# Clustered attention and two MLPs on one core: another order of the work of the first heads

## The chip, the core and the metric

The kernel runs on one core of one Trainium2 chip. The metric is the device time of one execution in microseconds (us). The engines are named as in the profile: PE is TensorE's matmul, PEld its load of weights, DVE is VectorE, ACT ScalarE, POOL GpSimd, SP SyncE, whose queue issues most DMAs. Each engine takes its instructions strictly in the order in which the program emits them.

## The reference, cut to what matters

```
q_assign = argmax(q_n . c_n); k_assign = argmax(k_n . c_n)      # 16 clusters per head, unit vectors
mask   = q_assign[:, :, :, None] == k_assign[:, :, None, :]
scores = where(mask, scale * (q @ k.T), -1e9)                   # 2 batches x 8 heads, seq 768, head_dim 64
attn   = exp(scores - max(scores)); attn /= sum(attn) + 1e-9
x      = (attn @ v) as [1536, 512]
x      = (g where h = x @ w_in, g = h * sigmoid(1.702 h)) @ w_out            # d_ff 2048
out    = (silu(x @ w_gate) * (x @ w_val)) @ w_out                            # d_ff 1536
```

## The kernel before

Sixteen (batch, head) pairs, here simply heads 0 to 15 as in the code, go through attention one after the other; then come the MLPs, which are dense matmuls. The change touches only heads 0 to 4, that is the first 60 us of 864.

What one head needs, with the names of the code:

- `load_qk(h)` (L309, SP queue) brings q and k, transposed, into one of four staging tiles. `hi_q`, `hi_k` (L321, L325, L326, on ACT) write their fp32r-rounded part into the operand tiles `q2(h)`, `k2(h)`, and `lo_q`, `lo_k` (L330, L336, on DVE, or on POOL where the call says so) write the remainder beside it. `extra_rows(i)` (L369, L370) is three POOL memsets that prepare the rows of an operand tile which hold the clusters and the maxima.
- `similar` (L431) is eight matmuls for one head, q and k against the centroids, into one tile of `ps_x`, which has a single buffer. `largest` (L451 to L460) and `assign` (L469 to L480) turn that, on DVE, into one-hot rows; the last step transposes half of the sequence at a time (L477) and two copies per half (L480, on the engines that the call names) put the rows into `q2(h)` and `k2(h)`.
- `smax(h, c, n, pool, tag)` is one matmul on those rows (L503) and one DVE maximum over its PSUM tile (L508), twelve times per head. They give an upper bound of the scores of a row; `mneg` (L519, DVE) and `mrow` (matmul L535, ACT copy L537, a small DMA L538) put its negative into `q2(h)`. For head 0 `mrow_at_once` does that in two halves without the DMA (L526, L530).
- `scores(h, c, n)` is two matmuls (L550) and one ACT exponential (L557); `pv(h, c)` (L566) is the product with the values, twelve matmuls. `ps_m` has two PSUM buffers, `ps_s` three, `ps_o` two. `keep_warm` (L353) issues matmuls on zeros.

The schedule is written out by hand: the order of emission is the order on each engine. In the loop over heads (L654 on), head h's twelve scores are mixed with the twelve `smax` of head h + 1, and then six `pv(h, c)` follow, with other work hung on their c. Head 0 is special: its scores come ahead of the loop, together with the first six `smax` of head 1. Then, in the loop at h = 0, ACT gets `hi_q(4)` and `hi_k(4)`, DVE gets `lo_q(4)` and `lo_k(4)` at c = 0, and then come the last six `smax` of head 1, two behind each of `pv(0, 0)` to `pv(0, 2)`. At c = 3 come `mneg(1)`, `similar([2])`, `mrow(1)`, `largest([2])` and `assign([2])`. The loop at h = 1 opens with the first `scores(1, ...)` and `smax(2, ...)`.

Of the kernel before, what the change touches and what calls it, by code (L numbers as in the profile page):

```python
# [25 lines left out]
def tile_cluster_attention_two_mlps(ctx: ExitStack, tc: tile.TileContext, qk, v, cen, w1, w2, wg, wv, w3, out):  # L26
    nc = tc.nc
    B, H, D, _, S = qk.shape
# [243 lines left out]
    with ExitStack() as att:  # L272
# [34 lines left out]
        def load_qk(h):  # L307
            b, hh = divmod(h, H)
            nc.sync.dma_start(out=stage[h % NST], in_=qk[b, hh])  # L309
# [9 lines left out]
        def hi_q(h):  # L319
            src = stage[h % NST][:, 0:1, :]  # L320
            nc.scalar.copy(q2(h)[0:D], src.to_broadcast([D, 2, S]))  # L321

        def hi_k(h):
            src = stage[h % NST][:, 1, :]
            nc.scalar.copy(k2(h)[0:D, 1, :], src)  # L325
            nc.scalar.copy(k2(h)[D:2 * D, 0, :], src)  # L326

        def lo_q(h, eng=nc.vector):
            t = q2(h)
            eng.tensor_tensor(  # L330
                out=t[D:2 * D, 0, :], in0=stage[h % NST][:, 0, :], in1=t[0:D, 0, :].bitcast(F32), op=ALU.subtract
            )

        def lo_k(h, eng=nc.vector):
            t = k2(h)
            eng.tensor_tensor(  # L336
                out=t[0:D, 0, :], in0=stage[h % NST][:, 1, :], in1=t[0:D, 1, :].bitcast(F32), op=ALU.subtract
            )
# [28 lines left out]
        def extra_rows(i):  # L367
            for t in (q2_t[i], k2_t[i]):
                nc.gpsimd.memset(t[D:MROW, 1, :].bitcast(F32), 0.0)  # L369
            nc.gpsimd.memset(k2_t[i][MROW:MROW + 1, 1, :].bitcast(F32), 1.0)  # L370
# [8 lines left out]
        for i in range(NC):  # L379
            nc.vector.memset(wd[:, :, i:i + 1], float(NC - i))  # L380
        nc.gpsimd.memset(v_t[0][:, :, D:D + 1], 1.0)
        for i in range(1, 4):
            extra_rows(i)


# [38 lines left out]
        def similar(hs):  # L424


            ps = ps_x.tile([128, HALF], F32, tag="x", name="sims")
            todo = [(i, a, j, h, n) for n in range(2) for j, h in enumerate(hs) for i in (1, 0) for a in (0, 1)]
            for at, (i, a, j, h, n) in enumerate(todo):
                o = LEAD + 128 * (h % H) - (64 * n + 32 * i + NC * j)  # L430
                nc.tensor.matmul(  # L431
                    out=ps,
                    lhsT=cs[:, (1 + i) * a, o:o + 128],
                    rhs=(q2, k2)[i](h)[:, 0, n * HALF:(n + 1) * HALF],
                    start=(at == 0),
                    stop=(at == len(todo) - 1),
                )
            return ps
# [53 lines left out]
        def do(steps):  # L492
            for _ in steps:
                pass
# [15 lines left out]
        def next_smax(h, todo):  # L510
            c, n = todo.pop(0)
            smax(h, c, n, *((ps_m, "m"), (ps_m, "m"), (ps_x, "x"))[(len(todo) + 1) % 3])
# [8 lines left out]
        def mrow_at_once(h, n, pl, tag):  # L521

            ps = pl.tile([128, 512], F32, tag=tag, name="mrow1")[MROW:MROW + 1, 0:HALF]
            for c in range(SC // 2):
                at = n * (SC // 2) + c
                nc.tensor.matmul(  # L526
                    out=ps[:, c * 128:(c + 1) * 128], lhsT=nr_t[h][:, at:at + 1].bitcast(F32), rhs=ident,
                    start=(c == 0), stop=(c == SC // 2 - 1), skip_group_check=True,
                )
            nc.scalar.copy(q2(h)[MROW:MROW + 1, 1, n * HALF:(n + 1) * HALF], ps)  # L530

        def mrow(h, pl=ps_x, tag="x"):

            ps = pl.tile([SC, 128], F32, tag=tag, name="mrow")
            nc.tensor.matmul(out=ps, lhsT=nr_t.pop(h), rhs=ident_r)  # L535
            row = sm_p.tile([SC, 128], F32R, tag="row", name="row")
            nc.scalar.copy(row, ps)  # L537
            nc.sync.dma_start(  # L538
                out=q2(h)[MROW:MROW + 1, 1, :].rearrange("p (c s) -> p c s", s=128).bitcast(F32), in_=row.bitcast(F32)
            )  # L540
# [3 lines left out]
        def scores(h, c, n):  # L544
            if n == 0:
                p_t[h, c] = p_p.tile([128, S], F32, tag="p", name="p")
            at = slice(n * HALF, (n + 1) * HALF)
            ps = ps_s.tile([128, 512], F32, tag="s", name="st")[:, 0:HALF]
            for a, rows in ((0, 2 * D), (1, MROW + 1)):
                nc.tensor.matmul(  # L550
                    out=ps,
                    lhsT=k2(h)[0:rows, a, c * 128:(c + 1) * 128],
                    rhs=q2(h)[0:rows, a, at],
                    start=(a == 0),
                    stop=(a == 1),
                )
            nc.scalar.activation(p_t[h, c][:, at], ps, ACTF.Exp, scale=scale)  # L557
# [66 lines left out]
        hi_k(2)  # L624
        hi_q(2)
        lo_k(2, nc.gpsimd)
        load_qk(4)
        for i, (c, n) in enumerate((c, n) for m in range(2) for n in range(2) for c in range(3 * m, 3 * m + 3)):
            smax(0, c, n, *((ps_m, "m"), (ps_m, "m"), (ps_s, "s"), (ps_s, "s"), (ps_s, "s"))[i % 5])
            keep_warm(1)  # L630
            if i == 5:
                mneg(0, slice(0, SC // 2))
        mrow_at_once(0, 0, ps_o, "o")
        mneg(0, slice(SC // 2, SC))
        sims = similar([1])
        for c in range(SC):
# [2 lines left out]
        do(assign([1], (nc.vector.tensor_copy, nc.gpsimd.tensor_copy)))  # L639
        lo_q(2, nc.gpsimd)  # L640
        mrow_at_once(0, 1, ps_o, "o")
        maxima = [(c, n) for c in range(SC) for n in range(2)]
        for c in range(SC):
            scores(0, c, 1)
            next_smax(1, maxima)
        hi_k(3)
        hi_q(3)
        lo_k(3, nc.gpsimd)
# [7 lines left out]
        for h in range(NH):  # L656
            more, ahead = h + 1 < NH, h + 4 < NH
            if h > 0:
                maxima = list(steps) if more else []
            for step in steps if h else ():  # L660
                scores(h, *step)
                if maxima:
                    next_smax(h + 1, maxima)
            if h == 0:
                load_qk(5)
            if ahead:
                hi_q(h + 4)
                if h == 0:
                    hi_k(h + 4)
            if 0 < h < NH - 1:  # L670
                mneg(h + 1)
            if h % 2 == 0 and 0 < h < NH - 3:
                do(assign([h + 2, h + 3]))
            if h == NH - 1:
                qk_stack.close()
                sp_p = pool(ctx, "sp", 5, side="right")
                g_p = pool(ctx, "gp", 3, side="right")
                w_pools.append(pool(ctx, "wd1", LATE, side="right"))
            for c in range(SC):
                pv(h, c)  # L680
                if more and c == 0:
                    if h > 0:
                        mrow(h + 1)
                    load_v(h + 1)
                    if ahead:
                        if h > 0:
                            hi_k(h + 4)
                        lo_q(h + 4)
                        lo_k(h + 4)
                        if h + 6 < NH:  # L690
                            load_qk(h + 6)
                        if h + 5 == NH:
                            qk1_stack.close()
                            stage_stack.close()
                            for to, t in zip((xh, xl), new_x(pool(ctx, "x1", 1, side="right"), 1)):
                                to.append(t)
                            w_pools.append(pool(ctx, "wd0", MID, side="right"))
                if h == 0:
                    for _ in range(min(2, len(maxima))):
                        next_smax(1, maxima)  # L700
                    if c == 3:
                        mneg(1)
                        sims = similar([2])
                        mrow(1, ps_o, "o")
                        do(largest([2], sims))
                        do(assign([2], (nc.scalar.copy, nc.vector.tensor_copy)))
                if h == 1 and c == 1:
                    do(largest([3], similar([3])))
                    do(assign([3]))
                if h > 0 and c == 0:  # L710
                    norm(h - 1)
                if h == NH - 1 and c > 0:
                    run([], [[("1", 0)], [("1", 1), ("2", 0)], [("1", 2)], [("2", 1)], []][c - 1], 0)
                take(takes.get((h, c), 0))
                if h == 1 and c == 4:
                    fetch_to(2)
                if h % 2:
                    if c == 2 and ahead:
                        do(largest([h + 3, h + 4], similar([h + 3, h + 4])))
                    if c in (3, 4) and h > 2:  # L720
                        to_x((h - 3) // 2, c - 3)
            if h == NH - 1:
                norm(h)
# [72 lines left out]
```

## Time and profile before

| | us |
|---|---|
| median of 3 runs | 865.94 (865.82 to 865.94) |
| the profiled execution, its own time | 865.92 |
| its span in the trace | 864.0 |
| PE busy in the span | 850.7 |
| DVE / ACT / POOL busy | 586.7 / 432.5 / 28.9 |

The profiled execution lies at the median, and its span is 1.9 us shorter than its time. Times in the rows are microseconds from the start of the span. Busy shares are means over stages with different limits; what the first heads are worth is read from their own stretch.

### The profile page before, as it was taken

What the parts mean: (1) busy time and instruction counts of PE and PEld (TensorE: products, weight loads), DVE (VectorE), ACT (ScalarE), POOL (GpSimd) and SP (SyncE); (2) the same over time, 40 slices, a digit from 0 to 9 for tenths busy, and PEclk for the clock granted to TensorE, in tenths of its full rate; (3) what the DMA queues carried; (4) which work ended last, traced back from release to release, by engine and by line L of the source; (5) the groups of instructions that cost most, each with busy time, mean ns of one, the idle gap of its engine ahead of it and who ended that gap; (6) DMA issues with size and microseconds to landing.
All of it is one profiled execution on the core that took longest, in us unless ns stands there. A gap on an engine that the chain in (4) does not pass through costs nothing.

```text
span 864.0 us, 12943 instructions
## 1 busy us (share of the span) xinstructions
PE 850.7 (98%) x5096; PEld 765.9 (89%) x5096; DVE 586.7 (68%) x1125; ACT 432.5 (50%) x819; POOL 28.9 (3%) x43
## 2 busy tenths in 40 slices
PE   8799999999999999999999999999999999999998
PEld 6699999999999988888888888888888888888886
DVE  7677878888896468888887767687774344333433
ACT  6546776676665445565664545564433233222322
POOL 9400000000000000000000000000000000000000
PEclk9889999999999999999999999999999999999999
DMA  5112222221122023333222222222200010000001
GB/s 114 34 27 71 90 54 56 60 51 50 35 81 76 1 84 112 109 111 119 101 74 82 67 97 74 74 74 75 96 1 1 1 49 25 1 1 1 0 1 74
DMA packets 26192, 49.73 MB, mean 58 GB/s; under 512 B 14522, under 2 KB 14612, under 8 KB 26132
## 3 DMA queue, kind: packets, MB, share of 16 engines
q1 hardware_dynamic: 25188, 47.14, 18.1%
q10 hardware_dynamic: 944, 1.77, 0.6%
q8 instruction: 40, 0.66, 0.3%
q14 instruction: 20, 0.16, 0.1%
HBM read 45.12 MB, written 3.15 MB: 56 GB/s over the span
## 4 chain that ended last, share of the span: by engine, by line
PE 94%; DVE 3%; POOL 2%; ACT 1%; issue 0%; DMA 0%; DVEq 0%; POOLq 0%; SPq 0%
PE h L156 39%; PE a L156 27%; PE pv L566 13%; PE st L550 7%; PE smax L503 4%; PE sims L431 3%; DVE nm L508 1%; PE xt L595 1%; POOL k L369 0%; POOL q L369 0%; POOL cs L365 0%; ACT q L321 0%; PE warm L353 0%; POOL k L370 0%; DVE oT L477 0%
## 5 line engine op out<-in xcount | busy, mean ns | idle before, releaser
L156 PE MATMUL h<-xh,sp 128*128 128x512 f32 (+1 forms) x1280 | 327.1, 337 | 0.1
L156 PEld LDWEIGHTS h<-xh,sp 128*128 128x128 f32 x1280 | 223.2, 189 | 28.4 <-issue 0.3
L156 PE MATMUL h<-xl,sp 128*128 128x256 f32 (+1 forms) x640 | 215.9, 337 | 0.0
L188 DVE SCALAR_TENSOR_TENSOR t<-t,h 128x512 f32<-128x512 f32 x112 | 61.9, 552 | 160.6 <-ACT t L185 160.6
L185 ACT ACTIVATE t<-h 128x512 f32<-128x512 f32 x112 | 54.6, 487 | 204.1 <-PE h L156 204.1
L156 PE MATMUL a<-g,sp 128*128 128x512 f32 (+1 forms) x768 | 139.4, 337 | 0.0
L566 PEld LDWEIGHTS pv<-v,p 128*128 128x128 f32 x1152 | 137.2, 195 | 0.2 <-issue 0.2
L566 PE MATMUL pv<-v,p 128*128 128x65 f32 x1152 | 136.6, 276 | 0.0
L156 PEld LDWEIGHTS a<-g,sp 128*128 128x128 f32 x768 | 119.9, 189 | 16.7
L156 PEld LDWEIGHTS h<-xl,sp 128*128 128x128 f32 x640 | 120.9, 189 | 14.4
L508 DVE TENSOR_REDUCE nm<-smax 128x1 f32<-128x384 f32 x192 | 100.6, 556 | 9.6 <-PE smax L503 9.5
L557 ACT ACTIVATE p<-st 128x384 f32<-128x384 f32 x192 | 90.8, 491 | 31.2 <-PE st L550 24.1
L156 PE MATMUL a<-sp,g 128*128 128x512 f32 x432 | 106.1, 390 | 0.0
L550 PE MATMUL st<-q,k 128*128 128x384 f32 (+1 forms) x384 | 98.6, 344 | 0.2 <-ACT q L530 0.2
L150 DVE TENSOR_TENSOR sp<-w,sp 128x512 fp32r<-128x512 f32 x136 | 92.9, 685 | 5.2 <-ACT sp L149 5.1
L156 PEld LDWEIGHTS a<-sp,g 128*128 128x128 f32 x432 | 79.5, 188 | 15.6
L149 ACT CAST sp<-w 128x512 fp32r<-128x512 f32 x136 | 83.1, 613 | 0.0
L503 PE MATMUL smax<-k,q 80*128 80x384 f32 x192 | 66.1, 346 | 7.3 <-DVE nm L508 4.4
L197 DVE TENSOR_TENSOR g<-t,g 128x512 fp32r<-128x512 f32 x112 | 62.1, 555 | 16.0 <-ACT g L194 11.5
L550 PEld LDWEIGHTS st<-q,k 128*128 128x128 f32 (+1 forms) x384 | 68.4, 190 | 2.1 <-ACT p L557 0.6
L194 ACT CAST g<-t 128x512 fp32r<-128x512 f32 (+1 forms) x48 | 24.7, 514 | 81.5 <-DVE t L193 81.5
L190 ACT CAST g<-t 128x512 fp32r<-128x512 f32 x64 | 32.9, 513 | 31.3 <-DVE t L188 31.3
(95 smaller groups left out, 663.6 us busy)
## 6 DMA issues: line engine op xcount, KB each, us to landing
raw<-in_w SPq DMA_DIRECT2D x44, 512.0 KB
raw<-in_wg SPq DMA_DIRECT2D x12, 512.0 KB
raw<-in_wv SPq DMA_DIRECT2D x12, 512.0 KB
st<-in_qk SPq DMA_DIRECT2D x15, 384.0 KB
v<-in_v SPq DMA_DIRECT2D x16, 192.0 KB
out<-osb ACTq DMA_DIRECT2D x6, 256.0 KB
out<-osb SPq DMA_DIRECT2D x6, 256.0 KB
q<-oT SPq DMA_DIRECT2D x6, 48.0 KB
```

Source lines behind the costliest of these rows:

```text
L149: lambda: nc.scalar.copy(t[:, 0, :], w),
L150: lambda: nc.vector.tensor_tensor(out=t[:, 1, :], in0=w, in1=t[:, 0, :].bitcast(F32), op=ALU.subtract),
L156: nc.tensor.matmul(out=out_ps, lhsT=lhs[a], rhs=rhs[b], start=(start and j == 0), stop=(stop and j == 2), **kw)
L185: nc.scalar.activation(t, hs[0], ACTF.Tanh, scale=tanh_scale)
L188: nc.vector.scalar_tensor_tensor(out=t, in0=t, scalar=1.0, in1=hs[0], op0=ALU.add, op1=ALU.mult)
L190: nc.scalar.copy(g[:, 0, at], t)
L197: nc.vector.tensor_tensor(out=g[:, 1, at], in0=t, in1=g[:, 0, at].bitcast(F32), op=ALU.subtract)
L503: nc.tensor.matmul(out=ps, lhsT=q2(h)[0:ONE + NC, 1, c * 128:(c + 1) * 128], rhs=k2(h)[0:ONE + NC, 1, n * HALF:(n + 1) * HALF],)
L508: nc.vector.tensor_reduce(out=nm_t[h][:, c, n:n + 1], in_=ps, axis=AX.X, op=ALU.max)
L550: nc.tensor.matmul(out=ps, lhsT=k2(h)[0:rows, a, c * 128:(c + 1) * 128], rhs=q2(h)[0:rows, a, at], start=(a == 0), stop=(a == 1),)
L557: nc.scalar.activation(p_t[h, c][:, at], ps, ACTF.Exp, scale=scale)
L566: nc.tensor.matmul(out=pv_t[h][:, i, :], lhsT=p[:, i * 128:(i + 1) * 128], rhs=v_t[h % 3][:, c, :], start=(c == 0 and i == 0), stop=(c == ...
```

## The change

It moves calls, and changes which PSUM tiles some of them use; no arithmetic is added or removed.

- Ahead of the heads: `extra_rows(3)` moves on POOL from behind `extra_rows(2)` to behind `lo_k(2)`, so behind head 0's `assign` copies. `mrow_at_once(0, 0)` moves into the loop of head 0's maxima, behind the tenth.
- `similar([2])` moves from c = 3 to c = 0, behind `pv(0, 0)`; the last six `smax` of head 1 stay two behind each of `pv(0, 0)` to `pv(0, 2)`, now in `ps_m` and `ps_s` tiles in turn and no longer in `ps_x`.
- `hi_q(4)`, `hi_k(4)`, `lo_q(4)`, `lo_k(4)` move to c = 3: the two of ACT behind `mrow(1)`, the two of DVE behind `assign([2])`.

```diff
         nc.gpsimd.memset(v_t[0][:, :, D:D + 1], 1.0)
-        for i in range(1, 4):
+        for i in range(1, 3):
             extra_rows(i)
...
         lo_k(2, nc.gpsimd)
+        extra_rows(3)
         load_qk(4)
...
                 mneg(0, slice(0, SC // 2))
-        mrow_at_once(0, 0, ps_o, "o")
+            if i == 9:
+                mrow_at_once(0, 0, ps_o, "o")
         mneg(0, slice(SC // 2, SC))
...
-        maxima = [(c, n) for c in range(SC) for n in range(2)]
-        for c in range(SC):
-            scores(0, c, 1)
-            next_smax(1, maxima)
+        maxima = list(steps)
+        for i in range(SC):
+            scores(0, i, 1)
+            smax(1, *maxima[i], *((ps_m, "m"), (ps_m, "m"), (ps_x, "x"))[i % 3])
...
-            if ahead:
+            if ahead and h > 0:
                 hi_q(h + 4)
-                if h == 0:
-                    hi_k(h + 4)
...
                         if h > 0:
                             hi_k(h + 4)
-                        lo_q(h + 4)
-                        lo_k(h + 4)
+                            lo_q(h + 4)
+                            lo_k(h + 4)
...
                 if h == 0:
-                    for _ in range(min(2, len(maxima))):
-                        next_smax(1, maxima)
+                    if c == 0:
+                        sims = similar([2])
+                    if c < 3:
+                        for i in (2 * c, 2 * c + 1):
+                            smax(1, *maxima[SC + i], *((ps_m, "m"), (ps_s, "s"), (ps_m, "m"), (ps_s, "s"))[i % 4])
                     if c == 3:
                         mneg(1)
-                        sims = similar([2])
                         mrow(1, ps_o, "o")
+                        hi_k(4)
+                        hi_q(4)
                         do(largest([2], sims))
                         do(assign([2], (nc.scalar.copy, nc.vector.tensor_copy)))
+                        lo_k(4)
+                        lo_q(4)
```

## Rows read from the trace of the kernel before

**Rows 1.** The page's first part: busy us (share of the span) xinstructions, by engine.

```profile
PE 850.7 (98%) x5096; PEld 765.9 (89%) x5096; DVE 586.7 (68%) x1125; ACT 432.5 (50%) x819; POOL 28.9 (3%) x43
```

**Rows 2.** Waits of PE, 0 to 130 us: total us, times, longest us.

```profile
PE smax L503 <- DVE nm L508: 4.4, 1, 4.4
...
PE smax L503 <- ACT q L480: 0.9, 1, 0.9
```

**Rows 3.** Busy us by stretch; after POOL come granted clock, DMA share, GB/s.

```profile
26.00:27.00 1.00, 0.56 (x2) 0.19 (x1) 0.94 (x3) 0.47 (x2) 0.48 (x1) 1.00 0.00 0
...
37.00:38.00 1.00, 0.00 (x0) 0.00 (x0) 1.00 (x2) 0.11 (x1) 0.95 (x3) 0.77 0.00 0
...
46.00:47.00 1.00, 1.00 (x5) 0.96 (x4) 0.00 (x0) 0.00 (x0) 0.00 (x0) 0.50 0.00 0
47.00:48.00 1.00, 1.00 (x8) 0.85 (x5) 0.58 (x1) 0.25 (x1) 0.00 (x0) 0.61 0.00 0
```

**Rows 4.** Timeline, 28 to 47 us: start, duration, engine, line, operation, out<-in [idle before].

```profile
30.41 0.33 PE L503 MATMUL smax<-k,q 80*128 80x384 f32 x1
...
32.68 2.85 ACT L321 CAST q<-st 64x1536 fp32r<-64x1536 f32 x2
...
35.43 0.83 ACT L325 CAST k<-st 64x768 fp32r<-64x768 f32 x1
35.55 1.28 DVE L330 TENSOR_TENSOR q<-st,q 64x768 fp32r<-64x768 f32 x1 [4.22 <-ACT q L321]
...
36.87 0.95 DVE L336 TENSOR_TENSOR k<-st,k 64x768 fp32r<-64x768 f32 x1
```

**Rows 5.** Chain that ended last, by time: start, us, what (x instructions merged).

```profile
53.23 0.18 PE smax L503
...
58.20 1.29 PE pv L566 x12
...
60.89 1.45 PE sims L431 x8
```

**Rows 6.** Timeline, 47 to 66 us, columns as in group 4.

```profile
47.15 0.31 PE L535 MATMUL mrow<-ident_r,nr 128*6 128x128 f32 x1
...
47.39 0.58 DVE L451 STREAM_TRANSPOSE T<-sims 128x384 f32<-128x384 f32 x1 [4.22 <-PE sims L431]
47.49 0.25 ACT L537 CAST row<-mrow 6x128 fp32r<-6x128 f32 x1 [10.38 <-PE mrow L535]
...
51.05 0.51 ACT L480 CAST q<-oT 16x384 fp32r<-16x384 f32 x1 [3.30 <-DVE oT L477]
...
51.61 0.45 PE L503 MATMUL smax<-k,q 80*128 80x384 f32 x1 [0.86 <-ACT q L480]
...
52.42 6.38 DVE L508 TENSOR_REDUCE nm<-smax 128x1 f32<-128x384 f32 x12
...
58.04 1.45 PE L566 MATMUL pv<-v,p 128*128 128x65 f32 x12
```

**Rows 7.** Timeline, 0 to 28 us, columns as in group 4.

```profile
12.42 0.65 DVE L473 TENSOR_SCALAR T<-T,s,s 128x192 f32<-128x192 f32 x1
...
13.77 1.06 ACT L480 CAST q<-oT 16x384 fp32r<-16x384 f32 x2 [1.14 <-POOL k L369]
13.81 0.73 POOL L370 MEMSET k<- 1x768 f32 x1
...
14.60 0.95 POOL L480 CAST k<-oT 16x384 fp32r<-16x384 f32 x2
...
15.15 0.44 PE L503 MATMUL smax<-k,q 80*128 80x384 f32 x1 [1.30 <-POOL k L480]
...
15.63 2.88 DVE L508 TENSOR_REDUCE nm<-smax 128x1 f32<-128x384 f32 x6 [1.34 <-PE smax L503]
...
25.31 0.38 DVE L473 TENSOR_SCALAR T<-T,s,s 128x192 f32<-128x192 f32 x1
...
26.52 0.61 POOL L480 CAST k<-oT 16x384 fp32r<-16x384 f32 x1 [5.25 <-DVE oT L477]
```

## The prediction

> **What bounds the kernel now.** I read the page's busy shares first: PE is busy for nearly the whole span [rows 1], so an edit pays only where PE waits or runs slowly. The waits of PE say where that is. All that it lists lie in the first 60 us, and two matter here: a `smax` held 4.4 us by DVE's maxima, and one held 0.9 us by ACT's copy of head 2's clusters [rows 2]. The busy time by stretch adds a third loss that no list of waits shows. Behind the 4.4 us wait the granted clock falls: 0.77 in 37 to 38, 0.50 up to 47, 0.61 in 47 to 48 [rows 3]. [...]
>
> The timeline gives the cause of the long wait. DVE was idle for 4.22 us behind ACT's copies for `hi_q(3)` and `hi_q(4)`, because `lo_q(4)` (L330) stands ahead of head 1's remaining maxima in its queue; it then spent 1.28 and 0.95 us on the two `lo` steps [rows 4]. PE, with no free PSUM tile for the next `smax`, stood still and lost its clock. Nothing of head 4 was wanted that early.
>
> **The change part by part.** I follow PE between four marks: A, the sixth `smax` of head 1 (30.41 [rows 4]); B, the product of `mrow(1)` (47.15); C, the first `smax` of head 2 (51.61); D, `pv(1, 0)` (58.04) [rows 6].
>
> *Up to A: `extra_rows(3)` out of the way.* Head 0's first `smax` (15.15) waited 1.30 us for POOL's copy at 14.60, which followed the memset of 13.81 directly, though ACT had the same transposed half at 13.77 [rows 7]. Without the three memsets POOL starts near 13.82 (a little behind ACT). In head 1's case, where DVE works beside it, such a copy takes 0.61 us, so `smax` starts near 14.49: 0.66 us gained. DVE's L473 may return more: 0.65 us beside POOL's memsets, 0.38 us beside none [rows 7], so another 0.27. I take both, 0.9 us, and keep 0.6 for the range. The memsets, about 0.73 each and 2.2 in all, go behind `lo_k(2)`; next on POOL are head 1's copies, ahead of which POOL had been idle for 5.25 us [rows 7]: nothing. Were that cover gone, they would cost head 1's chain up to 2.2. `mrow_at_once(0, 0)` moves ahead of four short matmuls; its maxima are there, the sum of PE's work is the same: nothing; below, 0.1 if the last `keep_warm` finds its buffer still read. A moves from 30.41 to 29.5, for head 1's chain follows with the same lengths.
>
> *A to B.* Before: 16.74 us. After, on PE: the sixth `smax`, `pv(0, 0)`, `similar([2])`, two `smax`, `pv(0, 1)`, two, `pv(0, 2)`, two, `pv(0, 3)`, and `mrow`. At the full clock a `pv` is 1.29, the eight similarities 1.45, a `smax` 0.18 [rows 5]: 4 x 1.29 + 1.45 + 7 x 0.18 = 7.87. `mrow` needs the last two maxima and `mneg`. DVE does a maximum every 0.48 us when fed (2.88 / 6 [rows 7]); starting some 0.45 behind their matmuls, two of them and a short `mneg` end about 0.15 us after `pv(0, 3)`. So 8.0, and 8.7 gained: the 4.4 wait and some 4.3 of slow clock. `similar` needs `lo_q(2)` from POOL and the one `ps_x` tile, which the sixth maximum frees; `pv(0, 0)` covers that. If it did not, PE would wait some tenths.
>
> *B to C.* Before: 4.46, DVE's chain from 47.39 to ACT's copy at 51.05, the copy, and `smax` [rows 6]. The chain is as long as before. It started with the end of the similarities, and now starts with the end of `mneg`; in both cases that is about when `mrow` runs, and `pv(0, 4)`, `pv(0, 5)` and two score matmuls lie beside it. This is why the similarities being early gains nothing of its own here: DVE can't start on them until the maxima queued ahead are through. New on ACT are `hi_k(4)`, `hi_q(4)`: they stand ahead of ACT's cluster copies. `mrow`'s product 0.31, the row copy 0.25 [rows 6], then 2 x 0.83 and 1.43 (half of 2.85 [rows 4]): done at B + 3.75 against DVE's chain at about B + 3.6. So the copy (0.51) ends near B + 4.3 and C is at B + 4.35: 0.1 gained, between 0.1 lost (the copies 0.2 slower) and 0.25 gained (ACT no limit). The wait in front of C stays, 0.9 to 1.2.
>
> *C to D, the new cost.* `lo_k(4)` and `lo_q(4)` now stand on DVE between `assign([2])` and head 2's maxima. PE waits for these, since only three PSUM tiles take `smax`. Before, DVE's first maximum started at 52.42, C + 0.81, and D was C + 6.43 [rows 6]. By the `lo` rows DVE is later by 2 x 0.95 = 1.9 (POOL is idle by then; beside POOL one took 1.28 [rows 4], so up to 2.5). The first maximum starts at C + 2.6 and ends 0.55 later; the fourth `smax` can go at C + 3.15. Before, it went at about C + 2.0 (three steps of 6.38 / 12 = 0.53, the second 0.3 late). So 1.2 us is lost, up to 1.8. From there DVE, at 0.48 a maximum against PE's 0.53 a step, catches up before `mneg(2)` is wanted, so `mrow(2)` waits no more than before; if it didn't, 0.35.
>
> *Moved past queues.* SP issues the same DMAs in the same order. The staging tile of head 4 comes free some 6 us later, and its next user is head 8, a long way on. From D on PE is full, and head 5's operands stand to it as before; nothing downstream gives the gain back.
>
> **The sum.** 0.9 + 8.7 + 0.1 - 1.2 = 8.5 us, made against the profiled execution, 865.92, practically the median 865.94: **857.4 us**. Its own range, by the ends above: 856.7 (L473 quicker still, ACT no limit) to 858.8 (start 0.6 only, `lo` at 2.5, 0.35 at `mrow(2)`).
>
> **The rivals.**
>
> *The clock falls again.* PE would have about 1 us of waiting before C and 1.2 to 1.5 us at the fourth `smax`, within some 4 us. Against a fall: in 26 to 27 PE was busy for 0.56 of the stretch, among several waits, and the clock stayed at 1.00; the 0.86 us in front of C left no mark either; the fall came behind 4.4 us of standing still [rows 2, 3, 6]. For it: the two waits lie closer together and are longer. Before, a low stretch was 10.2 us long, so it could cost up to 5.1; but here the dense stream of scores and `smax` follows, and before, the eight similarities, 2.9 us at that level, stood right ahead of its end, so 1.5 is the lower end. 858.9 to 862.5, most likely 860.
>
> [...]
>
> *The similarities do not get in beside the products.* If POOL, with the memsets now in its queue, were so late with head 1's copies or `lo_q(2)` that PE waits for it at `similar([2])`, the wait of DVE has only become one of POOL. POOL must lose more than 3 us of the idle 5.25, and each microsecond beyond costs one: 861 to 865.9.
>
> *Slower: the low clock stays through head 1's products.* Place: the fall happens at the fourth `smax` and the stream that follows doesn't lift it. It decides from 17 us at the lower level, half of which eats the 8.5. Eight steps at 1.06, two `pv` at 2.6 and the similarities at 2.9 make 16.6, so it must last into `pv(1, 2)`, against 10.2 before. Then 866 to 868.
>
> **How the numbers follow.** Forecast 0.76, clock 0.13, similarities late 0.05, slower 0.04, the rest (a wait not foreseen, of either sign) 0.02. The first two are faster, and so is nearly all of the third: faster by over 0.2% (1.7 us, about what a measurement of this kernel can tell from no change) 0.94, same 0.02, slower 0.04. The range runs from 856.6 to 860.5: the forecast's bounds and the likelier half of the clock's case.
>
> **What would show it.** Right: no wait of PE over 2 us; the granted clock at 1.00 in every microsecond from 30 to 60; DVE's maxima of head 1 done near 37 us; the first `smax` at 14.2 to 14.5; a wait of 1.2 to 1.5 us in front of head 2's fourth `smax`, put down to DVE; `pv(1, 0)` near 49.5 instead of 58.04. Wrong: a clock below 1.00 between 40 and 50, a wait at `similar([2])`, or waits of PE behind `pv(1, 0)` that the trace of before doesn't have.

## The result and the profile after

The changed kernel takes 857.41 us (857.32 to 857.5 over 4 executions) against 865.88 for the kernel before in the same measurement: a ratio of 0.9902, 95% interval 0.9885 to 0.9919. The forecast was 857.4, within 856.6 to 860.5.

| | before | after |
|---|---|---|
| median, us | 865.88 | 857.41 |
| profiled execution, its own time / its span | 865.92 / 864.0 | 857.43 / 855.5 |
| mark A, sixth `smax` of head 1 | 30.41 | 29.54 |
| mark B, product of `mrow(1)` | 47.15 | 37.57 |
| mark C, first `smax` of head 2 | 51.61 | 41.74 |
| mark D, `pv(1, 0)` | 58.04 | 49.50 |

The span is 8.5 us shorter, and at D the changed kernel is already 8.54 us ahead: all of the gain is made in the first 50 us. First the page's busy line of the changed kernel, then the list of PE's waits in 0 to 130 us; they answer to [rows 1] and [rows 2].

```profile
PE 846.1 (99%) x5096; PEld 761.4 (89%) x5096; DVE 585.8 (68%) x1125; ACT 432.7 (51%) x819; POOL 28.9 (3%) x43
```

And the waits (total us, times, longest us):

```profile
PE smax L503 <- DVE nm L508: 1.2, 1, 1.2
PE smax L503 <- ACT q L480: 1.2, 2, 0.9
```

PE has the same 5096 matmuls but is 4.6 us less busy: that is the part of the gain that no wait shows, matmuls that ran at the lower clock and now don't (a `pv` took 2.65 us at 38.83 in the kernel before, and takes 1.45 at 29.71 here). The 4.4 us wait is gone, and 1.2 us has come up under the same name. The busy time by stretch (after POOL: granted clock) shows both remaining waits with the clock at 1.00, where [rows 3] had 0.50:

```profile
41.00:42.00 1.00, 0.26 (x1) 0.26 (x2) 0.94 (x3) 0.68 (x3) 0.00 (x0) 1.00 0.00 0
...
44.00:45.00 1.00, 0.05 (x1) 0.05 (x1) 0.97 (x3) 0.27 (x1) 0.00 (x0) 1.00 0.09 16
```

The timeline of the changed kernel, from the start to mark D; these lines answer to [rows 4, 6, 7].

```profile
13.48 1.10 POOL L480 CAST k<-oT 16x384 fp32r<-16x384 f32 x2 [1.28 <-DVE oT L477]
...
14.16 0.41 PE L503 MATMUL smax<-k,q 80*128 80x384 f32 x1 [0.30 <-ACT q L480]
...
21.65 2.48 PE L550 MATMUL st<-q,k 128*128 128x384 f32 x12
...
25.64 0.61 POOL L480 CAST k<-oT 16x384 fp32r<-16x384 f32 x1 [3.04 <-DVE oT L477]
...
29.54 0.34 PE L503 MATMUL smax<-k,q 80*128 80x384 f32 x1
...
37.34 0.57 DVE L451 STREAM_TRANSPOSE T<-sims 128x384 f32<-128x384 f32 x1
...
37.57 0.22 PE L535 MATMUL mrow<-ident_r,nr 128*6 128x128 f32 x1
...
39.51 0.36 DVE L471 TENSOR_TENSOR T<-T,mx 128x192 f32<-128x192 f32 x1
...
39.68 1.48 ACT L321 CAST q<-st 64x1536 fp32r<-64x1536 f32 x1
...
40.99 0.35 DVE L480 CAST k<-oT 16x384 fp32r<-16x384 f32 x1
41.19 0.51 ACT L480 CAST q<-oT 16x384 fp32r<-16x384 f32 x1
...
41.74 0.45 PE L503 MATMUL smax<-k,q 80*128 80x384 f32 x1 [0.87 <-ACT q L480]
...
42.37 0.95 DVE L336 TENSOR_TENSOR k<-st,k 64x768 fp32r<-64x768 f32 x1
...
43.35 0.95 DVE L330 TENSOR_TENSOR q<-st,q 64x768 fp32r<-64x768 f32 x1
44.34 5.92 DVE L508 TENSOR_REDUCE nm<-smax 128x1 f32<-128x384 f32 x12
44.95 0.44 PE L503 MATMUL smax<-k,q 80*128 80x384 f32 x1 [1.21 <-DVE nm L508]
```

Read from the bottom: head 2's fourth `smax` waits 1.21 us for a PSUM tile, for DVE's maxima start only at 44.34, behind the two `lo` steps of head 4. The first `smax` waits 0.87 us for ACT's copy at 41.19, which started when `hi_q(4)` (39.68 + 1.48) let it.

### The profile page after: what moved, and what is told of

Same layout as the page of the kernel before. It is cut to its first block, busy times and chain, and to the rows that moved or that the text cites. A ratio compares the mean times of both kernels' runs of the same rounds, so it can differ in the third digit from the quotient of the medians.

```text
span 855.5 us, 12942 instructions
## 1 busy us (share of the span) xinstructions
PE 846.1 (99%) x5096; PEld 761.4 (89%) x5096; DVE 585.8 (68%) x1125; ACT 432.7 (51%) x819; POOL 28.9 (3%) x43
## 4 chain that ended last, share of the span: by engine, by line
PE 95%; DVE 4%; issue 0%; ACT 0%; DMA 0%; POOL 0%; DVEq 0%; POOLq 0%; SPq 0%; ACTq 0%
PE h L156 39%; PE a L156 27%; PE pv L566 13%; PE st L550 7%; PE smax L503 4%; PE sims L431 3%; DVE nm L508 1%; PE warm L353 1%; PE xt L595 1%; DVE oT L477 0%; DMA q<-oT 0%; DVE q L330 0%; DVE k L336 0%; DVE T L451 0%; DVE T L471 0%
## 5 line engine op out<-in xcount | busy, mean ns | idle before, releaser
L566 PEld LDWEIGHTS pv<-v,p 128*128 128x128 f32 x1152 | 134.3, 192 | 0.0
L566 PE MATMUL pv<-v,p 128*128 128x65 f32 x1152 | 134.0, 273 | 0.0
L508 DVE TENSOR_REDUCE nm<-smax 128x1 f32<-128x384 f32 x192 | 100.4, 556 | 10.3 <-PE smax L503 10.2
```

Source lines behind the costliest of these rows:

```text
L508: nc.vector.tensor_reduce(out=nm_t[h][:, c, n:n + 1], in_=ps, axis=AX.X, op=ALU.max)
L566: nc.tensor.matmul(out=pv_t[h][:, i, :], lhsT=p[:, i * 128:(i + 1) * 128], rhs=v_t[h % 3][:, c, :], start=(c == 0 and i == 0), stop=(c == ...
```

## The experiments

The theory: the gain comes from taking head 4's steps out of the way of head 1's maxima; the clock falls only behind the long standstill; the similarities' early place gains nothing; and the two `lo` steps are a new cost of 1.2 us. The main rival: the clock can fall behind the two short waits too. The kernels ran in three groups, each on one chip beside the kernel before.

### One part at a time

**Head 4's steps alone**, in the kernel before:

```diff
-            if ahead:
+            if ahead and h > 0:
                 hi_q(h + 4)
-                if h == 0:
-                    hi_k(h + 4)
...
                         mrow(1, ps_o, "o")
+                        hi_k(4)
+                        hi_q(4)
                         do(largest([2], sims))
                         do(assign([2], (nc.scalar.copy, nc.vector.tensor_copy)))
+                        lo_k(4)
+                        lo_q(4)
```

> The kernel before with one part of the change alone: head 4's hi and lo steps go behind head 1's maxima; the similarities of head 2 stay at c = 3, the start stays as it was. My theory: the lo step in DVE's queue is the sole cause of the 4.4 us wait and of the slow clock behind it, so both go. PE then reaches the similarities near 36.9, ends them at 38.3, and DVE's chain and ACT's copies (head 4's hi steps ahead of them) put the first maximum matmul of head 2 near 42.6 and pv(1, 0) near 50.3 instead of 58.0: 858.2 us, 0.8 above the full change, all of which is the start. Rival: the early similarities carry a part of the gain of their own: then 859 us or more here, with the wait in front of head 2's first maximum over 1.5 us.

Measured: 860.8 us (860.31 to 862.54), ratio 0.9945, interval 0.9928 to 0.9961. The 4.4 us wait is gone and the matmuls stand where they were expected: C at 42.73 (expected 42.6). But behind that wait the clock fell. First the timeline's line at C:

```profile
42.73 0.45 PE L503 MATMUL smax<-k,q 80*128 80x384 f32 x1 [1.12 <-ACT q L480]
```

The stretches (PE busy first, granted clock behind POOL):

```profile
42.00:43.00 1.00, 0.27 (x1) 0.27 (x2) 0.94 (x3) 0.51 (x1) 0.00 (x0) 1.00 0.00 0
43.00:44.00 1.00, 1.00 (x4) 0.64 (x4) 0.93 (x3) 0.81 (x2) 0.00 (x0) 0.62 0.00 0
...
49.00:50.00 1.00, 1.00 (x5) 1.00 (x4) 0.60 (x2) 0.49 (x1) 0.00 (x0) 0.50 0.00 0
50.00:51.00 1.00, 1.00 (x7) 1.00 (x6) 0.80 (x2) 0.58 (x2) 0.00 (x0) 0.97 0.00 0
```

A standstill of 1.12 us was followed by the fall, and PE stayed at the lower level from about 43.2 to 50. All four executions have a mean clock of 0.994 to 0.996, so all lost some of it; the profiled one shows where. So the long wait of before had the stated cause, but a wait of a quarter of its length can be followed by the same fall. The time fits the rival's bound of 859, by another mechanism than the one it named.

**The similarities alone**, with the tiles that their place needs; head 4's steps stay early:

```diff
-                    for _ in range(min(2, len(maxima))):
-                        next_smax(1, maxima)
+                    if c == 0:
+                        sims = similar([2])
+                    if c < 3:
+                        for i in (2 * c, 2 * c + 1):
+                            smax(1, *maxima[i], *((ps_m, "m"), (ps_s, "s"), (ps_m, "m"), (ps_s, "s"))[i % 4])
                     if c == 3:
                         mneg(1)
-                        sims = similar([2])
```

> The kernel before with the other part alone: head 2's similarities behind pv(0, 0), and the last six maxima of head 1 in ps_m and ps_s tiles in turn; head 4's hi and lo steps stay early on ACT and DVE, the start stays. If the wait of DVE is what costs, it is still there, DVE is at its first of these maxima at 37.8 as before; but PE now has the similarities (1.45 us), four maxima and two more pv to do before it lacks a PSUM tile: it stands still only from about 36.6 to 38.3, too short for the clock to fall. Then mneg ends near 40.9, head 2's first maximum matmul goes near 45.2 and pv(1, 0) near 51.6: 859.5 us. The two parts are then substitutes, each worth 6 to 8 us alone and 8 together. Rival, by my reading that the similarities are worth nothing in themselves: the wait and the slow clock remain, 864 to 866 us.

Measured: 862.38 us (862.18 to 863.45), ratio 0.9959, interval 0.9944 to 0.9974. PE's line in the timeline:

```profile
38.35 1.00 PE L503 MATMUL smax<-k,q 80*128 80x384 f32 x2 [1.55 <-DVE nm L508]
```

Its stretches, from the standstill to the end of the low level:

```profile
37.00:38.00 1.00, 0.00 (x0) 0.00 (x0) 1.00 (x2) 0.10 (x1) 0.95 (x3) 1.00 0.00 0
38.00:39.00 1.00, 0.65 (x2) 0.65 (x3) 1.00 (x3) 0.00 (x0) 0.49 (x1) 0.69 0.00 0
...
51.00:52.00 1.00, 1.00 (x4) 1.00 (x4) 0.58 (x2) 0.47 (x2) 0.00 (x0) 0.50 0.00 0
52.00:53.00 1.00, 1.00 (x7) 1.00 (x7) 0.91 (x2) 0.70 (x2) 0.00 (x0) 0.98 0.00 0
```

DVE is as late as before (the same 38.3), but PE had work until then and stood still for 1.55 us, not 4.4, as expected: each part alone takes away most of the same wait. "Too short for the clock to fall" was wrong, and here PE stayed low longer than before the change, to 52: three `pv` and the first scores of head 1 ran at that level.

**The start alone**: `extra_rows(3)` behind `lo_k(2)`, nothing else.

> The kernel before with only extra_rows(3) moved behind lo_k(2) on POOL. My theory: head 0's first maximum matmul goes at 14.2 instead of 15.15 and the head start of 0.9 us lasts to the end, since the long wait of PE later begins and ends earlier by the same: 865.0 us. Rival: the head start is absorbed by the long wait near 34 to 38 us (whose end is set by ACT's and DVE's steps for head 4): 865.9 us.

Measured: 865.1 us (864.42 to 866.45 over 10 executions) against 866.06 beside it: ratio 0.9987, interval 0.9977 to 0.9996. The medians differ by 0.96 us: the head start lasts to the end, as expected. The profiled execution does not show that part, for it was the slowest of the ten (866.45 us), with one more fall of the clock, near 27 us. It does show the start, the first `smax` and the first scores of head 0:

```profile
14.16 0.42 PE L503 MATMUL smax<-k,q 80*128 80x384 f32 x1 [0.32 <-ACT q L480]
...
21.51 2.47 PE L550 MATMUL st<-q,k 128*128 128x384 f32 x12
```

In the changed kernel the first `smax` goes at the same 14.16, but the scores at 21.65: `mrow_at_once(0, 0)` in its new place cost 0.14 us.

**The change without its start** (`extra_rows(3)` and `mrow_at_once(0, 0)` back where they were):

> The changed kernel with the start of before: extra_rows(3) ahead of head 0's copies, mrow_at_once(0, 0) behind the loop. It differs from the run with only head 4's steps moved by the place of head 2's similarities alone. If the early similarities are what keeps the wait in front of head 2's first maximum at 0.9 us and the clock up, 858.3 us at a clock of 1.0. If it is where the waits fall in time that decides on the clock, 860 to 861 us.

Measured: 859.04 us. It falls into two: 858.16 and 858.21 at a mean clock of 1.0, and 859.86 and 861.05 at 0.996 and 0.995. With the full clock it is the expected 858.3; with it or without is the question of the next group.

### Is the clock's staying up part of the change, or luck?

**The changed kernel again**, on two chips:

> The changed kernel itself, run again beside the others. In the two kernels with only one part of the change a wait of PE of 1.1 and 1.6 us was followed by the lower clock, which I had not expected, while the changed kernel kept the full clock with waits of 0.9 and 1.2 us. Theory: its waits are just short of what brings the clock down, in every execution: 857.4 us again, mean clock 1.0 throughout. Rival: it was luck, whether such a wait is followed by a fall varies from execution to execution: some executions near 860 us at a mean clock of 0.996.

> The changed kernel once more, beside the next two. Where its two waits stay at the full clock 857.4 us (or that plus what the start takes longer on this chip), about 860 in the executions in which the clock falls; by the earlier ones, 4 of 11 fell.

On one chip seven executions gave 857.01, 857.0 and 857.5 at a mean clock of 1.0, but 859.24, 860.37, 861.25 and 867.36 at 0.996, 0.995, 0.995 and 0.984; on the other four gave 857.06 to 857.32, all at 1.0 (median 857.14; ratio 0.9895, interval 0.988 to 0.991). With the first four that is 11 of 15 at the full clock; all four that fell ran on one chip, where they were 4 of 7. The one at 867.36 lies even in the range of the prediction's slower case, 866 to 868; it was not the profiled one, so where its clock fell is not known. The profile of the first of these chips was of the execution at 861.25: the waits in front of C and at the fourth `smax` are 0.87 and 1.23 us there too, and the clock falls at the second. Its list of waits, its timeline and its stretches, a line or a few of each:

```profile
PE sims L431 <- DVE k L336: 1.8, 1, 1.8
```

```profile
45.85 0.69 PE L503 MATMUL smax<-k,q 80*128 80x384 f32 x1 [1.23 <-DVE nm L508]
```

```profile
44.00:45.00 1.00, 0.62 (x4) 0.29 (x2) 0.97 (x2) 1.00 (x3) 0.00 (x0) 1.00 0.00 0
45.00:46.00 1.00, 0.15 (x1) 0.15 (x1) 0.97 (x3) 0.15 (x1) 0.00 (x0) 0.88 0.06 16
46.00:47.00 1.00, 1.00 (x4) 1.00 (x5) 1.00 (x3) 0.00 (x0) 0.00 (x0) 0.50 0.00 0
```

That is the prediction's rival, the clock falling again: the same program, the same two waits, and another clock. The first line, of the list of waits, is a separate loss: in this execution the first similarities waited 1.8 us for head 0's operands, where the changed kernel's first profile lists 0.3.

**The similarities late**, with the last six maxima of head 1 back in the tiles that go with that place; all the rest of the change is kept:

```diff
-                    if c == 0:
-                        sims = similar([2])
...
-                            smax(1, *maxima[SC + i], *((ps_m, "m"), (ps_s, "s"), (ps_m, "m"), (ps_s, "s"))[i % 4])
+                            smax(1, *maxima[SC + i], *((ps_m, "m"), (ps_m, "m"), (ps_x, "x"))[i % 3])
...
                         mneg(1)
+                        sims = similar([2])
                         mrow(1, ps_o, "o")
```

> The changed kernel with head 2's similarities back at c = 3 and the last maxima back in their old tiles; all the rest of the change stays. If the early similarities keep the clock up, the wait in front of head 2's first maximum is 1.1 us here and the clock falls behind it: 859.9 us. If not, 857.6 us: only the 0.2 us by which DVE's chain starts later is lost.

Measured: 860.19 us (859.59 to 861.58), and all five executions at a mean clock of 0.994 to 0.996. In the profile the chain of DVE starts 0.2 us behind `mrow`, where in the changed kernel it starts 0.23 us ahead of it:

```profile
37.64 0.22 PE L535 MATMUL mrow<-ident_r,nr 128*6 128x128 f32 x1
37.84 0.58 DVE L451 STREAM_TRANSPOSE T<-sims 128x384 f32<-128x384 f32 x1 [1.69 <-PE sims L431]
...
42.06 0.45 PE L503 MATMUL smax<-k,q 80*128 80x384 f32 x1 [1.12 <-ACT q L480]
```

With the run of head 4's steps alone, the late similarities make the wait in front of C 1.12 us, and all 9 executions lost some of the clock; with early ones it is 0.87 us, and 13 of 19 executions (the changed kernel and the one without its start) keep it. But all six that lost it ran on the chip of this run: there the early place fell in 6 of 11, the late one in 5 of 5, too few to tell apart, and in the two other measurements the early place fell in 0 of 8. So the early similarities are worth 0.25 us of waiting directly; that they keep the clock up is likely, but not shown. What it would be worth depends on that: 860.19 is 3.2 us above the changed kernel's executions at the full clock on this chip (857.0), but only 0.95 above its median there (859.24). What I can't separate is whether the length of that one wait does it, the tiles, the chip, or what else their place shifts.

**Matmuls on zeros in the two waits**, four and five of 0.22 us:

> The changed kernel with matmuls on zeros put into its two waits: four in front of head 2's first maximum matmul, five in front of its fourth, 0.22 us each, about as long as the waits. If the waits are what lets the clock fall, every execution keeps the full clock, 857.4 to 857.7 us, with no one near 860. If the clock falls for another reason (the products with few columns ahead of it, the stage as such), about as many executions near 860 us as for the changed kernel.

Measured: 857.24 us (856.99 to 857.55), all four executions at 1.0. But the changed kernel beside it on that chip had no fall either, so this does not tell the two apart. It shows only that PE's waits can be filled at hardly any cost, 0.1 us by the medians.

### The two remaining waits

**Head 4's `lo` steps on POOL**, in the same place of the program:

```diff
-                        lo_k(4)
-                        lo_q(4)
+                        lo_k(4, nc.gpsimd)
+                        lo_q(4, nc.gpsimd)
```

> The changed kernel with head 4's two lo steps on POOL instead of DVE, in the same place. My theory: they are what holds head 2's fourth maximum matmul for 1.2 us, DVE takes the maxima 1.9 us earlier and PE does not wait there: 856.2 us. Rival: POOL's two steps (1.8 us each) now run beside DVE's last steps of assign([2]), which read and write SBUF as they do, and slow these, so that the wait comes back in front of head 2's first maximum matmul: 857 to 858.5 us. The lengths of DVE's steps between 39.5 and 42.5 us tell.

Measured: 860.25 us (859.97 to 860.84), ratio 0.9933, interval 0.9918 to 0.9948: the rival was right in its mechanism, and its price of 857 to 858.5 too low, for it left the clock out. The timelines of POOL, DVE and PE, one after the other:

```profile
38.54 1.86 POOL L336 TENSOR_TENSOR k<-st,k 64x768 fp32r<-64x768 f32 x1 [1.26 <-ACT k L325]
40.93 1.80 POOL L330 TENSOR_TENSOR q<-st,q 64x768 fp32r<-64x768 f32 x1 [0.54 <-POOL k L336]
...
38.76 0.35 DVE L469 TENSOR_REDUCE mx<-T 128x12 f32<-128x192 f32 x1
39.15 1.47 DVE L471 TENSOR_TENSOR T<-T,mx 128x192 f32<-128x192 f32 x1
...
41.13 0.57 DVE L477 STREAM_TRANSPOSE oT<-T 64x384 f32<-64x384 f32 x1
41.74 1.21 DVE L480 CAST k<-oT 16x384 fp32r<-16x384 f32 x1
...
43.09 0.66 PE L503 MATMUL smax<-k,q 80*128 80x384 f32 x1 [2.58 <-DVE k L480]
```

And a stretch of that wait:

```profile
42.00:43.00 1.00, 0.00 (x0) 0.00 (x0) 0.97 (x2) 0.24 (x1) 0.73 (x1) 0.57 0.00 0
```

DVE's L471 took 1.47 us, 0.36 in the other kernels, and ended 0.2 us after POOL's first step did; its copy took 1.21 instead of 0.35 and ended 0.2 us after the second. Not every DVE step beside them ran long: L469, a reduction with one input from SBUF, took its 0.35 us beside POOL's first step, and the transpose L477 its 0.57 beside the second. L471 has two inputs from SBUF, the copy one; what sets the two that were held up apart from the two that were not, no run here shows. The wait in front of C is 2.58 us here, against 0.87; that and a fall of the clock more than ate the 1.2 us.

**The `lo` steps on POOL behind `assign([2])`**, by letting POOL also copy head 2's key clusters ahead of them:

```diff
-                        do(assign([2], (nc.scalar.copy, nc.vector.tensor_copy)))
-                        lo_k(4)
-                        lo_q(4)
+                        do(assign([2], (nc.scalar.copy, nc.gpsimd.tensor_copy)))
+                        lo_k(4, nc.gpsimd)
+                        lo_q(4, nc.gpsimd)
```

> The changed kernel with POOL copying head 2's key clusters and then doing head 4's lo steps, so behind the steps of assign([2]) that they blocked, beside maxima only. My theory: the lo steps on DVE cost 1.2 to 1.4 us at head 2's fourth maximum matmul, and that wait goes: 856.1 us where the clock is full. The wait in front of the first maximum matmul, 0.9 us, stays, for ACT's hi steps still stand ahead of its copy. Rival: the price of the lo steps comes back as a block of DVE's maxima: 857.4 us.

Measured: 856.11 us (856.0 to 856.25), clock 0.999 to 1.0; ratio 0.9884, interval 0.9867 to 0.99. Same steps, same engine, 1.85 and 1.83 us long, but now beside maxima, which read PSUM and are not slowed (12 in 6.43 us, against 6.38 before, beside nothing [rows 6]). Whether it is PSUM that spares them or that they are reductions with one input, like L469 above, these runs don't tell.

```profile
41.83 0.41 PE L503 MATMUL smax<-k,q 80*128 80x384 f32 x1 [0.96 <-ACT q L480]
...
42.20 1.85 POOL L336 TENSOR_TENSOR k<-st,k 64x768 fp32r<-64x768 f32 x1
42.28 6.43 DVE L508 TENSOR_REDUCE nm<-smax 128x1 f32<-128x384 f32 x12 [0.72 <-PE smax L503]
...
44.12 1.83 POOL L330 TENSOR_TENSOR q<-st,q 64x768 fp32r<-64x768 f32 x1
```

The price of the two `lo` steps on DVE is 857.14 - 856.11 = 1.03 us by the medians of this chip; the wait that goes is 1.21. The wait in front of C stays, as expected; it is 0.96 us, and in the profiled execution the clock stayed up behind it (mean 1.0), though on a chip on which the changed kernel didn't fall either.

**Both waits away**: head 3's `hi` steps early on ACT, head 4's where head 3's were, `largest([2])` directly behind its similarities, and the edit above.

```diff
         lo_k(2, nc.gpsimd)
+        hi_k(3)
         extra_rows(3)
...
+        hi_q(3)
         sims = similar([1])
...
-        hi_k(3)
-        hi_q(3)
+        hi_k(4)
+        hi_q(4)
         lo_k(3, nc.gpsimd)
...
                         sims = similar([2])
+                        do(largest([2], sims))
...
-                        hi_k(4)
-                        hi_q(4)
-                        do(largest([2], sims))
```

> The changed kernel with both remaining waits taken away: head 3's hi steps go early on ACT (behind hi_q(2) and head 0's first mrow), head 4's hi steps where head 3's were, largest([2]) runs directly behind similar([2]), ahead of the last six maxima, POOL copies head 2's key clusters and then does head 4's lo steps, beside maxima only. By the trace of the changed kernel DVE is idle for 2.35 us there and 0.67 us twice, so the four steps of largest (1.6 us) cost the maxima nothing; assign([2]) then ends ahead of PE: 1.1 us less in front of head 2's first maximum matmul, and 1.3 less at its fourth: 855.0 us, full clock. Rival: POOL's lo steps block DVE again as in the run with them beside assign([2]), or the early largest delays mneg(1) and with it mrow(1): 857 us or more.

> The kernel without the two waits once more: 2.4 us under the changed kernel's executions at the full clock, 855.0 us, and no execution with the lower clock between 40 and 50 us, so that the median difference is larger than 2.4 where the changed kernel falls.

Measured: 855.02 us (854.93 to 856.47; ratio 0.9869, interval 0.9856 to 0.9882) on the chip on which the changed kernel had a median of 859.24, and 854.84 (854.54 to 854.92; ratio 0.9868, interval 0.9853 to 0.9882) on the other, beside 857.14. The expected 855.0 was met: 2.0 and 2.3 us under the changed kernel's executions at the full clock (857.0 and 857.14). The low clock is not wholly gone: on the first chip one of the four executions took 856.47 us at a mean clock of 0.998, 1.4 us above the other three; it was not profiled, so where it lost them is not known. The profile of the second lists no wait of PE over 0.4 us behind the start. Its timeline from ACT's copy to `pv(1, 0)`, which stood at 49.50 in the changed kernel's first profile and at 49.20 in the one on this chip:

```profile
39.22 1.11 ACT L480 CAST q<-oT 16x384 fp32r<-16x384 f32 x2 [1.12 <-DVE oT L477]
...
40.73 0.34 PE L503 MATMUL smax<-k,q 80*128 80x384 f32 x1
41.10 6.42 DVE L508 TENSOR_REDUCE nm<-smax 128x1 f32<-128x384 f32 x12 [1.31 <-PE smax L503]
...
46.77 1.45 PE L566 MATMUL pv<-v,p 128*128 128x65 f32 x12
```

It is the fastest version of this study.

## Why the prediction was right, and where it was not

- **What bounds it.** Right. The wait of DVE on `hi_q(4)`, and the clock behind it, were what the change took away; the similarities or head 4's steps alone each took away most of the wait.
- **Up to A.** 0.9 predicted, 0.87 in the profile, and in part by luck. The first `smax` went at 14.16, 0.99 us earlier (0.66 + 0.27 were forecast). `mrow_at_once(0, 0)`, put at nothing, took back 0.14 us. The start alone gave 1.0 us by the medians.
- **A to B.** 8.0 predicted, 8.03 measured (29.54 to 37.57).
- **B to C.** 4.35 predicted, 4.17 measured. ACT set C, as forecast, and was through with `hi_q(4)` at B + 3.59; the terms given for that add up to 3.65, not to the 3.75 that stands there. I had DVE's chain start "about when `mrow` runs" in either place of the similarities; with the early place it starts 0.23 us ahead of `mrow`, with the late one 0.2 behind, and then it is DVE and not ACT that sets C. "The similarities being early gains nothing of its own here" is the step that failed: it gains 0.25 us of waiting, and all nine executions without it lost some of the clock. The same edit was judged by its cover alone, not by the wait that it shortens.
- **C to D.** 7.63 predicted (6.43 + 1.2), 7.76 measured. The wait came where it was forecast, at the fourth `smax`, 1.21 us, and with the two `lo` steps out of the way it went.
- **The clock.** The forecast had it stay up, and in all four executions of the result it did, but the argument was too weak, and that it came true there was partly luck. I took the 0.56 of 26 to 27 [rows 3] and the 0.86 us wait [rows 6] as evidence that such waits leave the clock alone; they are one execution. Waits of 1.12 and 1.55 us were followed by a fall in other kernels, and 0.87 with 1.2 in 4 of 15 executions of this one, 4 of 7 on one chip and none in the two other measurements. On that one chip the median was 859.24, above the forecast's own 856.7 to 858.8, though in the range. By all 15 the chance of that rival would be about 0.27, not 0.13; its price, 860 most likely, was right for most of them (859.24, 860.37, 861.25; the fourth, 867.36, lies outside). The low stretch of 10.2 us that its upper end of 862.5 starts from is read off the granted clock of the kernel before [rows 3], between 1.00 and 0.50: 0.46 us of 37 to 38, the nine up to 47, which are all at 0.50, and 0.78 of 47 to 48.
- **The range.** Its lower bound of 856.7 does not come out of the ends that it names: ACT no limit is worth 0.15 us, and no row prices "L473 quicker still". No execution of the changed kernel was below 857.0.
- **Queues.** POOL idle time covered the moved memsets, as told: it was idle 3.04 us in front of head 1's copies, against 5.25 before, and nothing downstream took the gain back.

## What to carry to other kernels

When an in-order engine holds a step that waits for something nobody needs yet, all that stands behind it in that queue is late (in the kernel before, DVE was idle for 4.22 us in front of such a step, with head 1's maxima behind it); look at the idle time in front of such a step, and at who waits for what is queued behind. Moving work to another engine pays only at a place where its steps don't hold up what runs beside them: beside the last steps of `assign([2])` the same two steps on POOL made the kernel nearly 3 us slower (860.25 us against 857.41 in another measurement, a fall of the clock included), and beside the maxima they gained 1 us. And a short wait of PE can cost more than its length: remove it even where it looks like 1 us, because the clock may fall behind it, as it did here, to 0.50, behind waits of 1.12, 1.23 and 1.55 us. One profile is no evidence that it doesn't.

## What the runs showed of the hardware that was not expected

- A fall of the granted clock needs no long standstill: 1.12 and 1.55 us of waiting were followed by 0.50 for some 7 and 14 us. In the profile of the kernel with only the start moved it fell even among the short waits near 27 us, each under half a microsecond:

```profile
27.00:28.00 1.00, 0.84 (x4) 0.84 (x5) 0.69 (x2) 0.48 (x1) 0.92 (x2) 0.85 0.00 0
28.00:29.00 1.00, 1.00 (x5) 1.00 (x4) 0.76 (x2) 0.49 (x1) 1.00 (x1) 0.50 0.00 0
```

- The same program gets another clock in another execution: the changed kernel 857.0 and 861.25 on one chip. Why is open, and so is the chip's part in it; filling the waits came beside executions in which nothing fell.
- POOL steps with two SBUF inputs, of 1.86 and 1.80 us, held up a DVE step of 0.36 us to 1.47 and a copy of 0.35 to 1.21; a reduction with one SBUF input took its 0.35 beside the first, and a transpose its 0.57 beside the second.
